# Linear attention and gated feed-forward: 23 identity products in the opening, and other slots for the attention work of the first looped pass

## Chip, cores and metric

One core of one Trainium2 chip. The metric is the device time of one execution in microseconds (us), the median over runs of the same program. A profile of one execution comes with it; its span is the time from its first to its last instruction.

## What is computed

Two stages, in float32:

```
state = 0                                   # per batch and head, 48 x 48
for t in range(768):                        # 4 batches, 8 heads of 48
    y[t]  = r[t] @ (state + (u * k[t]) outer v[t])
    state = w[t][:, None] * state + k[t] outer v[t]
x   = y as 3072 tokens x 384
out = (sigmoid(x @ w_gate) * (x @ w_val)) @ w_out      # 384 -> 1536 -> 384
```

## The kernel before, in words

**Groups and passes.** The 768 time steps of each batch are cut into 6 chunks of 128. A group q (0 to 23) is one chunk of one batch: batch q % 4, chunk q // 4. The four groups of one chunk make 512 tokens, which the feed-forward stage takes as one pass n (0 to 5). The 1536 hidden columns are 12 blocks f of 128.

**Attention work of a group.** `load_pin` and `load_tok` (L295, L304) fetch its two inputs by SyncE's queue into two buffers each, so a load waits until the group two places earlier has let go of its buffer. `bonus1`, `bonus2` and `bonus4` run on GpSimd (L317, L321, L328), `bonus3` on VectorE (L324). `prep_k` and `prep_r` (L334, L353) are scans and products on VectorE; `fade` (L347) scales the carried state. `guard` (L363) is ScalarE and reads what both scans wrote: `eg` has a single buffer. `turn_k` (L367) transposes the prepared keys on TensorE, `take_k` (L372) copies them out to `kT`, a single buffer. `section1` (L443) does the scores and sums on TensorE; `mask`, `middle` and `keep` (L456, L463, L471) follow on VectorE; `section2` (L448), or in the loops the weighing inside `both`, finishes the group. `take_y`, `turn_x`, `take_x`, `rest_x` turn the result into the feed-forward's operand, as a rounded part and a rest.

**Feed-forward step.** For each block f: `gate` (9 TensorE products of 128x128 by 512 columns, L525 and L528), `sigmoid` on ScalarE, `value` (9 products), `hidden` on VectorE (L545), `hidden_hi` on ScalarE (L549), `hidden_lo` on VectorE (L553), and, one step later, `down` (9 products, L568).

**Opening.** The class `Plan` simulates an order from costs given by hand for groups 0 to 7, for the twelve weight blocks (each is fetched and rebuilt from 64-bit words on VectorE, L269 to L287) and for pass 0. `section1(0)` and `section1(1)` lie in this part. Each engine runs its instructions in the order in which they are traced.

**Loops.** Passes 1 to 5 are written out as 12 steps of 4 slots; a dictionary `todo` hangs attention work on slots. Slot 0 comes ahead of `gate`, slot 1 ahead of `value`, slot 2 ahead of `down` of the step before, slot 3 behind it. `FIRST` gives the slots at which groups 8 to 11 are visited in pass 1. A visit `both(q)` does the end of group q and the scores and sums of group q+1 on TensorE, then `take_y(q)`, then mask, middle and keep of q+1, and it issues the loads of group q+2. `EARLY` holds, for each visit of pass 1, the slots at which group q+1 is prepared: first bonus1, bonus2, prep_k and fade; then turn_k and take_k; then prep_r and guard; then bonus3 and bonus4. In later passes the visits lie at slots 7, 19, 31 and 43 of the pass and these four at 7, 5, 3 and 3 slots ahead of the visit. Group 8 has turn_k at slot 1 and section1 at slot 3 of pass 1. Pass 1 also splits the last four weight blocks at slots 1 and 2, 5 and 6, 9 and 10, 13 and 14: `w_hi` (L284) on ScalarE, `w_lo` (L287) on VectorE.

```
row = 4 * NFF
start = (R0 + 1) * B
visit = {q: (q - start) // B * row + (7 + 12 * (q % B) if q >= start + B else FIRST[q - start]) for q in range(start, NG)}
at(1, turn_k, start)
at(1, take_k, start)
at(3, section1, start)
```

Of the kernel before, what the change touches and what calls it, by code (L numbers as in the profile page):

```python
# [9 lines left out]
F32 = mybir.dt.float32  # L10
# [11 lines left out]
P = 128  # L22
# [19 lines left out]
LATE = dict(b3=-1.05, wl=-28.0, xl=26.5)  # L42
ROOM = dict(pin=2, tok=2, bon=2, eg=1, ready=2, mid=1, kT=1, at=2, pair=1, bank=1, x=2, temp=1, pg=1, pu=1, unit=2)
R0 = 1
FIRST = [11, 21, 32, 43]
EARLY = [(4, 6, 8, 8), (12, 16, 17, 17), (23, 27, 28, 28), (34, 38, 39, 39)]
HC = C // 2
HALVES = [slice(0, HC), slice(HC, C)]
HW = 3 * DM // 2
# [155 lines left out]
def tile_kernel(ctx: ExitStack, tc: tile.TileContext, dec: bass.AP, tok: bass.AP, wts: bass.AP, u: bass.AP, out: bass.AP):  # L205
    nc = tc.nc
# [5 lines left out]
    ps1 = own.enter_context(tc.tile_pool(name="ps1", bufs=1, space=PSUM))  # L212
# [6 lines left out]
    def att_pair(name):  # L219
        return ps1.tile([P, 2, 512], F32, tag="pair", name=name)  # L220

    ident = const.tile([P, P], F32, name="ident")
# [85 lines left out]
    def kk(q):  # L308
        return pin[q][:, WW:WW + NP * C].rearrange("a (p c) -> a p c", c=C)

    def rr(q):
        return pin[q][:, WW + NP * C:].rearrange("a (p c) -> a p c", c=C)
# [63 lines left out]
    def values(q, p, o, half):  # L376
        h = 2 * p + o
        return tk[q][half, 2 * DM + h * D:2 * DM + (h + 1) * D]

    def scores(q):  # L380


        t = bank["a", q]
        todo = []
        for p in range(NP):
            for s, half in enumerate(HALVES):
                for o in range(2):
                    sl = slice(64 * o, 64 * o + D)
                    todo.append(lambda p=p, half=half, o=o, sl=sl: nc.tensor.matmul(  # L389
                        t[half, o, p * HC:(p + 1) * HC], lhsT=kk(q)[sl, p, half], rhs=rr(q)[sl, p, half], start=True, stop=True,  # L390
                        skip_group_check=True))
        return todo

    def sums(q):
        t = bank["a", q]
        todo = []
        for p in range(NP):
            for s, half in enumerate(HALVES):
                if s and q >= NG - B:
                    continue  # L400
                for o, m in ((0, 64), (1, D)):
                    todo.append(lambda p=p, s=s, half=half, o=o, m=m: nc.tensor.matmul(  # L402
                        t[64 * o:64 * o + m, s, NP * HC + p * D:NP * HC + (p + 1) * D],
                        lhsT=kT[q][half, p * L + 64 * o:p * L + 64 * o + m],
                        rhs=values(q, p, o, half), start=True, stop=True, skip_group_check=True))
        return todo
# [32 lines left out]
    def go(todo):  # L439
        for f in todo:  # L440
            f()

    def section1(q):  # L443

        bank["a", q] = att_pair(f"pa{q}")
        go(scores(q) + sums(q))

    def section2(q):  # L448


        t = att_pair(f"py{q}")
        bank["y", q] = [t[:, o, :NP * D].rearrange("a (p e) -> a p e", e=D) for o in range(2)]
        bank["yy", q] = t[:, :, :NP * D].rearrange("a o (p e) -> a o p e", e=D)
        go(among(*states(q, bank["y", q])) + among(*mix(q, bank["y", q])))
# [155 lines left out]
    for q in range(ahead + 2):  # L610
# [17 lines left out]
        add(f"tk{q}", "PE", 0.4, [f"pk{q}"], k + 0.1, turn_k, q, take=["bank", "kT"])  # L628
        add(f"kT{q}", "ACT", 0.53, [f"tk{q}"], k + 0.1, take_k, q, give=["bank"])
        add(f"s1_{q}", "PE", 1.3, [f"kT{q}", f"tok{q}", f"pr{q}"], k + 0.15, section1, q, take=["pair"], give=["kT"])  # L630
        add(f"mid{q}", "DVE" if old else "ACT", 0.36, [f"s1_{q}", old and f"fade{q}"], k + 0.1, middle, q, take=["mid"])
        add(f"mk{q}", "DVE", 0.7, [f"s1_{q}", f"b4_{q}"], k + 0.12, mask, q)
# [26 lines left out]
    for g, (i0, i1) in enumerate(GROUPS + [(0, B)]):  # L659
        m, some = i1 - i0, tall if g < 2 else WIDE  # L660
        for f in some:
            e = g == 0 or g == 1 and f in EXACT
            a, name = (0, f, i0, i1, e), f"{g}_{f}"
# [51 lines left out]
    def at(time, f, *a):  # L715
        todo.setdefault(time, []).append((f, a))

    def prepare(q, early, turn, late, more):
        at(early, bonus1, q)
        at(early, bonus2, q)  # L720
        at(early, prep_k, q)
        at(early, fade, q)
        at(turn, turn_k, q)
        at(turn, take_k, q)
        at(late, prep_r, q)
        at(late, guard, q)
        at(more, bonus3, q)
        at(more, bonus4, q)
# [8 lines left out]
# [5 lines that stand above are left out]
    settle(start, 3)  # L742
    for q, time in visit.items():
        if q + 1 < NG:
            prepare(q + 1, *EARLY[q - start] if q < start + B else (time - 7, time - 5, time - 3, time - 3))
        at(time, both, q)
# [78 lines left out]
```

## Time and profile before

| | before |
|---|---|
| runs, us | 582.59, 583.19, 584.51 (median 583.19) |
| profiled execution, us | 585.22 |
| its span, us | 582.9 |
| mean granted TensorE clock | 0.991 |
| TensorE products busy | 547.9 us, 94% |
| VectorE busy | 324.0 us, 56% |
| ScalarE busy | 204.7 us, 35% |
| GpSimd busy | 100.7 us, 17% |
| moved by DMA | 50.57 MB |

The profiled execution took 2.3 us more than its span, and 2.03 us more than the median of the runs. PE is TensorE's products, DVE VectorE, ACT ScalarE, POOL GpSimd, SPq SyncE's queue of DMA issues. Busy shares are means over stages with different limits; L numbers are lines of the kernel. In a timeline a line gives the start, the time until the end of the last of the merged instructions, and in square brackets how long the engine had been idle and what released it.

### The profile page before, as it was taken

Reading aid. Unit: us, or ns where it says so; the run is one execution under the profiler, and the core shown is the slowest. Engines: PE = TensorE matmul, PEld = TensorE weight load, DVE = VectorE, ACT = ScalarE, POOL = GpSimd, SP = SyncE. Lnnn points to the kernel's source line nnn. Section 1 sums busy time; section 2 is a strip of 40 time slices with the busy share of each in tenths; the row PEclk is TensorE's granted clock in tenths of the full one; section 3 lists DMA queues with packets and bytes.
Section 4 is the critical chain, followed back from the end, with each engine's and each line's share of the span. In section 5 each row is a group of like instructions: output and inputs, shape, how many; then the busy total and the mean of one; then the engine's idle time right before and its main releaser. Section 6 shows DMA issues by size and latency. Waiting matters only on the chain.

```text
span 582.9 us, 13165 instructions
## 1 busy us (share of the span) xinstructions
PE 547.9 (94%) x5864; PEld 449.3 (77%) x5864; DVE 324.0 (56%) x451; ACT 204.7 (35%) x376; POOL 100.7 (17%) x89
## 2 busy tenths in 40 slices
PE   3698899999889999999999999999999999999995
PEld 2577687887767888877888888888888888888884
DVE  4998999996754654644535545645545521222221
ACT  2557765744432323422223333223323322321221
POOL 4350533104010210210121221211220200000000
PEclk9999999999898999999999999999999999999998
DMA  8748827324020232231130330230330200100001
GB/s 253 256 170 284 251 93 305 76 77 147 12 90 15 76 89 60 84 90 40 51 90 12 110 113 13 77 90 15 112 107 19 72 3 1 55 1 1 0 1 60
DMA packets 11044, 50.57 MB, mean 87 GB/s; under 512 B 1265, under 2 KB 1266, under 8 KB 9442
## 3 DMA queue, kind: packets, MB, share of 16 engines
q1 hardware_dynamic: 8818, 45.70, 25.0%
q10 hardware_dynamic: 2160, 3.93, 1.7%
q8 instruction: 48, 0.79, 0.6%
q14 instruction: 18, 0.15, 0.1%
HBM read 44.91 MB, written 4.72 MB: 85 GB/s over the span
## 4 chain that ended last, share of the span: by engine, by line
PE 86%; DVE 6%; DMA 3%; issue 2%; ACT 1%; POOL 1%; SPq 0%; DVEq 0%; ACTq 0%
PE po L568 24%; PE pg L525 16%; PE pu L525 15%; PE pg L528 8%; PE pu L528 8%; PE py L431 3%; PE py L418 3%; DMA pin<-dec 3%; PE pg L522 2%; PE pk L370 2%; PE pa L389 2%; PE pa L402 1%; PE px L481 1%; DVE raw L275 1%; PE po L564 1%
## 5 line engine op out<-in xcount | busy, mean ns | idle before, releaser
L545 DVE TENSOR_TENSOR sg<-pu,sg 128x512 f32<-128x512 f32 (+1 forms) x76 | 50.3, 661 | 166.8 <-PE pu L528 162.1
L568 PE MATMUL po<-hh,w 128*128 128x512 f32 x408 | 130.3, 401 | 0.0
L525 PE MATMUL pg<-x,w 128*128 128x512 f32 x408 | 107.5, 399 | 0.0
L525 PE MATMUL pu<-x,w 128*128 128x512 f32 x408 | 105.0, 393 | 0.0
L525 PEld LDWEIGHTS pu<-x,w 128*128 128x128 f32 x408 | 76.8, 189 | 16.2
L525 PEld LDWEIGHTS pg<-x,w 128*128 128x128 f32 x408 | 74.9, 188 | 16.2
L568 PEld LDWEIGHTS po<-hh,w 128*128 128x128 f32 x408 | 75.1, 190 | 14.2
L549 ACT CAST hh<-sg 128x512 fp32r<-128x512 f32 x68 | 42.2, 620 | 123.0 <-DVE sg L545 122.9
L538 ACT ACTIVATE sg<-pg 128x512 f32<-128x512 f32 (+1 forms) x76 | 43.5, 572 | 115.2 <-PE pg L528 110.8
L568 PE MATMUL po<-hl,w 128*128 128x512 f32 x204 | 80.2, 393 | 0.1
L553 DVE TENSOR_TENSOR hl<-sg,hh 128x512 fp32r<-128x512 f32 x68 | 50.2, 738 | 42.2 <-ACT hh L549 42.2
L319 POOL TENSOR_TENSOR bon<-tok,ub 128x384 f32<-128x384 f32 x24 | 30.7, 1280 | 237.1 <-DMA tok<-tok 170.7
L528 PE MATMUL pg<-x,w 128*128 128x512 f32 x204 | 58.3, 394 | 0.0
L528 PE MATMUL pu<-x,w 128*128 128x512 f32 x204 | 57.6, 390 | 0.0
L332 POOL TENSOR_TENSOR at<-eye,a 128x512 f32<-128x512 f32 x24 | 31.5, 1314 | 126.2 <-DVE a L326 126.2
L568 PEld LDWEIGHTS po<-hl,w 128*128 128x128 f32 x204 | 38.6, 189 | 9.2 <-DVE hl L553 0.6
L528 PEld LDWEIGHTS pg<-x,w 128*128 128x128 f32 x204 | 38.7, 190 | 8.4
L528 PEld LDWEIGHTS pu<-x,w 128*128 128x128 f32 x204 | 38.3, 188 | 8.0
L339 DVE TENSOR_TENSOR_SCAN eg<-pin,ends 112x516 f32<-112x516 f32 x24 | 34.7, 1446 | 9.5 <-DMA pin<-dec 9.5
L365 ACT ACTIVATE eg<-eg 112x1032 f32<-112x1032 f32 x24 | 25.6, 1067 | 31.1 <-DVE pin L361 29.8
L322 POOL TENSOR_TENSOR bon<-bon,tok 128x384 f32<-128x384 f32 x24 | 35.5, 1480 | 1.9
L476 ACT COPY bon<-py 128x384 f32<-128x384 f32 x24 | 11.5, 478 | 63.7 <-PE py L431 63.7
(78 smaller groups left out, 646.5 us busy)
## 6 DMA issues: line engine op xcount, KB each, us to landing
pin<-dec SPq DMA_DIRECT2D x23, 675.5 KB, 5.9
tok<-tok SPq DMA_DIRECT2D x24, 576.0 KB, 5.8
raw<-wts SPq DMA_DIRECT2D x12, 1152.0 KB, 10.6
y<-o ACTq DMA_DIRECT2D x15, 256.0 KB, 2.0
y<-o SPq DMA_DIRECT2D x3, 256.0 KB, 3.2
pin<-dec SPq DMA_DIRECT2D x1, 448.0 KB, 3.8
pin<-dec SPq DMA_DIRECT2D x1, 227.5 KB, 2.8
line<-u SPq DMA_DIRECT2D x1, 1.5 KB
```

What stands on the lines that cost most here:

```text
L319: nc.gpsimd.tensor_tensor(out=bon[q], in0=tk[q][:, 0:DM], in1=ub, op=ALU.mult)
L322: nc.gpsimd.tensor_tensor(out=bon[q], in0=bon[q], in1=tk[q][:, DM:2 * DM], op=ALU.mult)
L332: nc.gpsimd.tensor_tensor(out=att[q], in0=eye.unsqueeze(1).unsqueeze(1).broadcast_to(shape), in1=a0, op=ALU.mult)
L339: nc.vector.tensor_tensor_scan(out=e[:, 516:0:-1], data0=t[:, 516:0:-1], data1=ends[:, 516:0:-1], initial=0.0, op0=ALU.mult, op1=ALU.add,)
L365: nc.scalar.activation(both, both, AF.Square, accum_out=acc_d[:, q:q + 1])
L525: nc.tensor.matmul(t, lhsT=w[f][:, cols], rhs=x[n][:, a, k, spot], start=k == 0 and j == 0, stop=False)
L528: nc.tensor.matmul(t, lhsT=whi[f][:, cols], rhs=x[n][:, 1, k, i0 * C:i1 * C], start=False, stop=k == NKT - 1)
L538: nc.scalar.activation(sg, hid["g", n, f, i0], AF.Sigmoid)
L545: nc.vector.tensor_tensor(out=sg, in0=hid["u", n, f, i0], in1=sg, op=ALU.mult)
L549: nc.scalar.copy(hh, hid["s", n, f, i0])
L553: nc.vector.tensor_tensor(out=hl, in0=hid["s", n, f, i0], in1=hid["hi", n, f, i0].bitcast(F32), op=ALU.subtract)
L568: nc.tensor.matmul(to, lhsT=w[f][:, cols], rhs=h, start=first and i == 0, stop=last and i == 2, skip_group_check=True)
```

## The change

Behind `section1` of groups 0 and 1, eleven and twelve products of the 128x128 identity with itself are issued into a bank (`po0`) that nothing reads until pass 0's first `down` starts a new sum there. In pass 1 the visits of groups 8, 9, 10 and 11 move from slots 11, 21, 32, 43 to slots 7, 19, 31, 43, and the preparation of groups 9 to 12 moves with them.

```diff
-FIRST = [11, 21, 32, 43]
-EARLY = [(4, 6, 8, 8), (12, 16, 17, 17), (23, 27, 28, 28), (34, 38, 39, 39)]
+BUSY = {0: 11, 1: 12}
+FIRST = [7, 19, 31, 43]
+EARLY = [(0, 2, 4, 4), (11, 14, 16, 16), (23, 26, 28, 28), (35, 38, 40, 40)]
...
         bank["a", q] = att_pair(f"pa{q}")
         go(scores(q) + sums(q))
+        if q in BUSY:
+            t = ps1.tile([P, 512], F32, tag="po0", name=f"busy{q}")
+            for _ in range(BUSY[q]):
+                nc.tensor.matmul(t[:, :P], lhsT=ident, rhs=ident, start=True, stop=True)
```

## Rows read from the trace of the kernel before

**Rows 1.** The page: granted clock in 40 slices; the chain's shares.
```profile
PEclk9999999999898999999999999999999999999998
...
PE 86%; DVE 6%; DMA 3%; issue 2%; ACT 1%; POOL 1%; SPq 0%; DVEq 0%; ACTq 0%
```

**Rows 2.** Windows: us; PE, PEld, DVE, ACT, POOL busy; PEclk, DMA share, GB/s.
```profile
153.00:157.00 4.00, 4.00 (x13) 3.33 (x14) 3.32 (x5) 1.05 (x2) 0.00 (x0) 0.57 0.01 4
...
175.50:181.00 5.50, 5.45 (x19) 4.45 (x20) 3.56 (x4) 2.12 (x4) 1.05 (x1) 0.69 0.01 3
181.00:262.00 81.00, 79.97 (x959) 65.83 (x958) 42.28 (x62) 23.31 (x47) 13.54 (x11) 1.00 0.25 75
262.00:576.00 314.00, 312.76 (x2921) 257.45 (x2919) 132.48 (x202) 85.57 (x164) 37.31 (x28) 1.00 0.15 46
```

**Rows 3.** Waits of TensorE over the whole span: total, times, longest.
```profile
PE py L431 <- issue: 3.4, 3, 1.3
```

**Rows 4.** Timeline of TensorE, pass 0's end and pass 1.
```profile
122.85 0.55 PE L370 MATMUL pk<-ident,pin 112*128 112x112 f32 x4
...
125.42 0.26 PE L418 MATMUL py<-ready,pin 48*64 48x48 f32 x2
...
152.95 0.95 PE L370 MATMUL pk<-ident,pin 112*128 112x112 f32 x4 [1.92 <-issue]
...
157.04 1.53 PE L525 MATMUL pg<-x,w 128*128 128x512 f32 x6
...
175.55 0.60 PE L370 MATMUL pk<-ident,pin 112*128 112x112 f32 x4 [3.12 <-DVE x L514]
...
181.74 0.62 PE L568 MATMUL po<-hh,w 128*128 128x512 f32 x2
...
199.01 0.55 PE L370 MATMUL pk<-ident,pin 112*128 112x112 f32 x4
...
203.53 0.62 PE L568 MATMUL po<-hh,w 128*128 128x512 f32 x2
```

**Rows 5.** Timeline of VectorE, then one line of GpSimd and of ScalarE, pass 1.
```profile
145.64 0.69 DVE L545 TENSOR_TENSOR sg<-pu,sg 128x512 f32<-128x512 f32 x1 [4.38 <-ACT sg L538]
...
150.83 1.22 DVE L339 TENSOR_TENSOR_SCAN eg<-pin,ends 112x516 f32<-112x516 f32 x1
...
152.18 0.66 DVE L345 TENSOR_TENSOR pin<-pin,eg 112x512 f32<-112x512 f32 x1
...
169.95 1.23 DVE L339 TENSOR_TENSOR_SCAN eg<-pin,ends 112x516 f32<-112x516 f32 x1 [3.55 <-DMA pin<-dec]
...
194.57 1.50 DVE L345 TENSOR_TENSOR pin<-pin,eg 112x512 f32<-112x512 f32 x1
...
194.51 1.01 POOL L319 TENSOR_TENSOR bon<-tok,ub 128x384 f32<-128x384 f32 x1 [14.29 <-DMA tok<-tok]
...
158.26 1.07 ACT L365 ACTIVATE eg<-eg 112x1032 f32<-112x1032 f32 x1 [3.47 <-DVE pin L361]
```

**Rows 6.** SyncE's queue (groups 9 and 10's loads), and the first one's landing.
```profile
136.86 28.39 SPq L301 DMA_DIRECT2D pin<-dec  x2
...
pin<-dec SPq DMA_DIRECT2D x1, 675.5 KB, 7.0
```

**Rows 7.** Timeline of TensorE, opening.
```profile
15.86 0.98 PE L370 MATMUL pk<-ident,pin 112*128 112x112 f32 x4 [5.20 <-DVE pin L345]
...
19.91 0.90 PE L481 MATMUL px<-ident,bon 128*128 128x128 f32 x3 [0.60 <-ACT bon L476]
...
25.92 1.09 PE L418 MATMUL py<-mid,pin 48*64 48x48 f32 x16 [3.23 <-DVE state L473]
...
48.24 0.49 PE L481 MATMUL px<-ident,bon 128*128 128x128 f32 x3
```

**Rows 8.** Timeline of VectorE, opening: the longest waits from 22 us on.
```profile
22.84 0.73 DVE L458 COPY_PREDICATED at<-after,pa 128x512 f32<-128x512 int32 x1 [1.08 <-PE pa L402]
...
52.77 1.23 DVE L339 TENSOR_TENSOR_SCAN eg<-pin,ends 112x516 f32<-112x516 f32 x1 [1.51 <-DMA pin<-dec]
```

## The prediction

> **What bounds the kernel now.** I read the chain first, then TensorE's waits, then the windows around each wait, then the other engines' timelines there. The chain is TensorE for 86% of the span [rows 1]. From 262 to 576 us its products are busy 312.76 of 314 us, from 181 to 262 us 79.97 of 81 [rows 2]; what is missing there is two of the three waits of L431 marked "issue", 3.4 us in all three [rows 3]. So whatever TensorE gains before 181 us moves the end by as much. Two stretches of pass 1 stand out, each a pause and then a slow clock:
> - 1.92 us ahead of turn_k(9) at 152.95 [rows 4]. VectorE finishes prep_k(9) just then: its scan starts at 150.83 and its product ends at 152.18 + 0.66 = 152.84 [rows 5]. Behind it the granted clock is 0.57 on the mean of 153 to 157 us [rows 2], that is, mostly the lower of its two levels, 1.2 instead of 2.4 GHz.
> - 3.12 us ahead of turn_k(10) at 175.55 [rows 4]. Here prep_k(10) began only at 169.95, after 3.55 us of waiting for its load [rows 5], and VectorE's queue did the rest. The clock behind it is 0.69 from 175.5 to 181 us [rows 2].
>
> The opening has the other pauses: 5.20 us ahead of turn_k(1) at 15.86 and 3.23 us ahead of section2(1) at 25.92 [rows 7]. The granted-clock line shows full speed there [rows 1], but three transposes take 0.90 us at 19.91 and 0.49 at 48.24 [rows 7], so by durations TensorE runs at its lower level through this stretch.
>
> **Pass 1: the visit of group 8 from slot 11 to 7, the preparation of 9 from (4, 6, 8, 8) to (0, 2, 4, 4), of 10 from (12, 16, 17, 17) to (11, 14, 16, 16).** No instruction is added or dropped; each visit's TensorE work is moved, not changed.
> - The pause at 152.95 goes: 1.92. Its slow clock: from turn_k(9) to the next gate 157.04 - 152.95 = 4.09 us for four transposes and nine products of down; the same work takes 125.42 - 122.85 = 2.57 at full clock [rows 4]. Saved 1.52.
> - The pause at 175.55 goes: 3.12. Its slow clock: turn_k, gate and value take 181.74 - 175.55 = 6.19, against 203.53 - 199.01 = 4.52 [rows 4]. Saved 1.67.
> - What is late next at turn_k(9). Its place is now right behind value(0), which is over when hidden(0) starts at 145.64; VectorE had idled 4.38 us before that [rows 5], so prep_k(9) and fade(9) fit there. But the load of group 9, issued at 136.86, lands 7.0 us later [rows 6], at 143.86. prep_k takes 152.84 - 150.83 = 2.01 and so ends at 145.87. I book a new wait of 0.5. hidden(0) slips behind prep_k and fade; its result is wanted by down(0), a whole gate and value later. take_k(9) must also wait for section1(8), which still reads the single kT buffer: that holds ScalarE for about a microsecond while its next work, sigmoid(1), has no input yet. Nothing.
> - What is late next at turn_k(10). Load 10 goes out with the visit, a step earlier than before, and has more than a step until slot 11: its 3.55 us of waiting goes. prep_k(10) stands on VectorE behind hidden(2), hidden_lo(2), rest_x(8) and w_lo(2), and is over, by the order above, some 0.4 us before value(3). I book 0 and keep 0.8 as the upper bound.
> - prep_r(9), bonus3(9), the mask of 9 and ScalarE's guard(9) stand a step earlier; their cover is the nine-product sums of TensorE beside them, and if it is gone the price is the last rival's. SyncE's loads of groups 10 and 11 move ahead with the visits and pass nothing else on that queue. GpSimd's two bonus products of 9 only waited for their load before and still do. The visits of 9, 10 and 11 move by 2, 1 and 0 slots into the pattern of the later passes, which run without pauses [rows 2]: nothing.
>
> Sum of pass 1: -1.92 - 1.52 - 3.12 - 1.67 + 0.5 = -7.7.
>
> [...] The product of prep_k took 0.66 alone and 1.50 where GpSimd's bonus product ran beside it, from 194.51 on [rows 5]. [...] Slot 0 puts both of group 9's there, but both hang on loads that land apart, so I leave it at 0.66; were they to meet, the new wait would be 1.50 - 0.66 = 0.84 longer, 1.3 instead of 0.5.
>
> **The opening: 11 and 12 products of 128 columns.** Nothing in the trace has this form. The nearest are the transposes by the identity, 0.90 / 3 = 0.30 each at the lower level, 0.49 / 3 = 0.16 at the upper [rows 7]. Eleven are 3.3 us in a pause of 5.20: hidden by the wait for prep_k(1). Twelve are 3.6 us in one of 3.23, hidden by the wait for keep(1), with 0.4 sticking out, or 2.0 at the upper level with nothing sticking out. Cost 0, bound 0.4. The bank is next written after the pauses, on the same engine.
>
> What a higher clock from there is worth is bounded by VectorE, which from 22 us on, until TensorE has the lead, waits only twice for over a microsecond: 1.08 us at 22.84 for section1(1)'s sums, and 1.51 at 52.77 for a load that is issued when TensorE lets a buffer go [rows 8]. Everything else that TensorE does faster before 33 us ends in front of a VectorE instruction that does not move. So the gain lies between 0 (or -0.4, the overhang) and 1.08 + 1.51 = 2.6. I take 1.0, the first wait: it is the nearest behind the first fill.
>
> Code-loading waits (the three of L431): the instruction stream shifts by 23 products, and such a wait may come or go, up to 1.3 each way [rows 3]. I take 0.
>
> **Sum.** -7.7 - 1.0 = -8.7. Against the profiled execution, 585.2, that is 576.5; it stands 2.03 above the median of the runs, so for the median 583.19 - 8.7 = 574.5.
>
> **Rivals.**
> 1. The identity products raise nothing that counts: the clock stays low until pass 0's dense products, or VectorE does not move. For it: dense small products already filled TensorE between the pauses and left it at the lower level. Against: these are full 128x128 products. 583.19 - 7.7 = 575.5.
> 2. One pause is moved, not removed: turn_k(9) waits longer for its load, or turn_k(10) for VectorE behind w_lo(2), long enough that the clock falls again. A pause of 1.92 had that effect, with 1.52 behind it [rows 4]. It costs 1.92 + 1.52 - 0.5 = 2.9: 577.4. For it: the margins are 0.5 and 0.4. Against: later passes keep the same distances.
> 3. Slower. At slot 4 guard(9) now stands on ScalarE ahead of sigmoid(1), and guard waits for prep_r on VectorE; before it waited 3.47 us there [rows 5]. If prep_r comes so late that sigmoid(1) frees the gate's bank after value(1), TensorE stops at each of the four visits of pass 1. At a pause and slow clock of 1.92 + 1.52 = 3.4 each, 13.8 in all, less 8.7: about 588. It decides from a delay of some 2 us, the length of value, and turns the sign at 2.2 us lost per visit. Against: guard stands the same way in the later passes, which show no pause.
>
> **How the numbers follow.** Forecast 0.45, 574.5; rival 1 0.30, 575.5; rival 2 0.20, 577.4; rival 3 0.05, 588. Low end: all of pass 1 without the new wait, 8.2, 2.6 in the opening and one code wait gone, 1.0: 583.2 - 11.8, about 571.5. High end: no gain in the opening, the first pause's 1.52 not in every run, both new waits (0.5 + 0.8) and a code wait of 1.3: 583.2 - 8.2 + 4.1, about 579. That holds all but rival 3 and some of rival 2's tail. A measurement tells 0.3% (1.7 us) from no change. Faster by more 0.95, within it 0.01, slower 0.04. The Trainium skill (TensorE: Matmul & The Clock Gate, Part 1) adds that one kernel met the faster clock after different numbers of products in different runs; by that the 1.52 and the opening's gain may vary from run to run. The runs before lie 1.9 us apart, which does not speak against it.
>
> **What would show it.** Right: no wait over 1 us at turn_k(9) and turn_k(10), clock 1.00 through pass 1, the pass shorter by 7 to 8 us; the transposes of group 0 near 0.49 instead of 0.90; VectorE's wait for section1(1) gone. Wrong: a pause at turn_k(9) with clock 0.5 behind it; sigmoid(1) late behind guard(9); transposes in the opening still at 0.90. A time under 571 would mean that the opening is not bound by VectorE as I read it; over 580, that the pauses moved on.

## The result and the profile after

The changed kernel takes 575.96 us (median of 4 runs, 575.17 to 577.14) against 582.89 of the kernel before on the same chip (4 runs, 582.03 to 584.51): 6.9 us less. The ratio on record is 0.9858, 95% interval [0.982, 0.9896], which is 8.3 us of the 583.19 that the prediction started from; the two medians alone give 0.9881, and the interval takes in both. Forecast were 574.5 and a range of 571.5 to 579.0. Timed again later beside other kernels, the ratio was 0.9858 [0.9819, 0.9897]. The profiled execution took 575.17 us with a span of 573.1; that of the kernel before had 582.9.

A line of the changed kernel's page, the clock by slices:

```profile
PEclk9799999999999999999999999999999999999999
```

Against [rows 1] the dip of the clock in the eleventh to thirteenth slice is gone, and a new one stands in the second slice, in the opening. The windows of the changed kernel (from:to and width in us; busy PE, PEld, DVE, ACT, POOL; PEclk, DMA share, GB/s) show both:

```profile
22.00:28.00 6.00, 6.00 (x47) 5.84 (x46) 4.95 (x6) 3.33 (x7) 0.70 (x1) 0.51 0.61 145
...
139.30:150.30 11.00, 10.55 (x110) 8.45 (x109) 7.38 (x12) 6.01 (x10) 1.77 (x2) 1.00 0.31 109
150.30:162.00 11.70, 11.70 (x203) 9.67 (x202) 7.27 (x13) 6.61 (x11) 2.09 (x2) 1.00 0.37 113
162.00:180.00 18.00, 17.38 (x228) 14.12 (x227) 11.98 (x16) 5.71 (x10) 3.27 (x3) 1.00 0.13 37
180.00:262.00 82.00, 82.00 (x822) 67.58 (x820) 44.28 (x65) 25.37 (x50) 15.57 (x12) 1.00 0.22 66
```

In pass 1 the clock is 1.00 throughout, where [rows 2] had 0.57 and 0.69. TensorE is missing 0.45 us of the window from 139.30 and 0.62 of that from 162.00. TensorE's waits in the changed kernel, over the whole span, name them (total, times, longest):

```profile
PE pa L403 <- issue: 2.7, 1, 2.7
PE pg L527 <- ACT sg L543: 1.4, 1, 1.4
...
PE py L432 <- issue: 1.0, 1, 1.0
...
PE pk L371 <- PE pu L533: 0.6, 1, 0.6
...
PE pk L371 <- ACT kT L375: 0.5, 1, 0.5
```

The two pauses of 1.92 and 3.12 [rows 4] have become 0.5 and 0.6. The waits of L431, now L432, are one of 1.0 instead of three of 3.4 [rows 3]. A wait of 2.7 in section1(1) is new, and so is one of 1.4 for the first sigmoid of pass 0: the faster TensorE of the opening gets there ahead of ScalarE. TensorE's timeline in the changed kernel (start, us, operation, the wait before it in brackets), first in the opening, then around pass 1:

```profile
10.60 4.42 PE L451 MATMUL busy<-ident 128*128 128x128 f32 x22
14.96 0.57 PE L371 MATMUL pk<-ident,pin 112*128 112x112 f32 x4
...
17.97 0.55 PE L486 MATMUL px<-ident,bon 128*128 128x128 f32 x3 [0.60 <-ACT bon L481]
...
18.96 0.32 PE L403 MATMUL pa<-tok,kT 64*64 64x48 f32 x9
21.98 0.88 PE L403 MATMUL pa<-tok,kT 64*64 64x48 f32 x23 [2.69 <-issue]
22.79 5.34 PE L451 MATMUL busy<-ident 128*128 128x128 f32 x24
28.06 0.67 PE L419 MATMUL py<-mid,pin 48*64 48x48 f32 x16
...
121.29 0.55 PE L371 MATMUL pk<-ident,pin 112*128 112x112 f32 x4
...
144.42 0.60 PE L371 MATMUL pk<-ident,pin 112*128 112x112 f32 x4 [0.45 <-ACT kT L375]
...
166.28 0.57 PE L371 MATMUL pk<-ident,pin 112*128 112x112 f32 x4 [0.62 <-PE pu L533]
...
194.68 0.61 PE L573 MATMUL po<-hh,w 128*128 128x512 f32 x2
```

The opening reads in this order: the first fill raises the clock (transposes 0.55 us instead of 0.90 [rows 7]); then TensorE stops for 2.69 us in the middle of a group of equal products; the clock falls, and the second fill runs at the lower level for 5.34 us, until section2(1) starts at 28.06 instead of 25.92 [rows 7].

Between the same two places, turn_k at 121.29 and the down sum at 194.68, lie 73.39 us. In the kernel before they were 203.53 - 122.85 = 80.68 [rows 4]. So 7.3 us of this pair of executions came from the visits of pass 1. Until the first of these places the changed kernel was 1.56 us ahead, and one code wait of the kernel before, 1.27 us, lies in that stretch. Two of its three lie behind 181 us, where the changed kernel has one.

### The profile page after: what moved, and what is told of

Read it like the earlier page. It is cut to its first block, busy times and chain, and to the rows that moved or that the text cites. A ratio compares the mean times of both kernels' runs of the same rounds, so it can differ in the third digit from the quotient of the medians.

```text
span 573.1 us, 13259 instructions
## 1 busy us (share of the span) xinstructions
PE 548.7 (96%) x5910; PEld 452.3 (79%) x5910; DVE 325.0 (57%) x451; ACT 204.3 (36%) x376; POOL 104.2 (18%) x89
## 4 chain that ended last, share of the span: by engine, by line
PE 83%; DVE 9%; issue 2%; ACT 2%; DMA 1%; POOL 1%; SPq 0%; ACTq 0%; DVEq 0%; POOLq 0%
PE po L573 23%; PE pg L530 16%; PE pu L530 15%; PE pu L533 8%; PE pg L533 8%; PE py L432 3%; PE py L419 3%; PE pa L403 1%; PE pa L390 1%; PE pk L371 1%; DMA tok<-tok 1%; DVE temp L273 1%; PE px L486 1%; DVE raw L276 1%; PE busy L451 1%
## 5 line engine op out<-in xcount | busy, mean ns | idle before, releaser
L558 DVE TENSOR_TENSOR hl<-sg,hh 128x512 fp32r<-128x512 f32 x68 | 51.9, 763 | 42.3 <-ACT hh L554 42.2
L320 POOL TENSOR_TENSOR bon<-tok,ub 128x384 f32<-128x384 f32 x24 | 29.2, 1215 | 230.5 <-DMA tok<-tok 199.2
L323 POOL TENSOR_TENSOR bon<-bon,tok 128x384 f32<-128x384 f32 x24 | 39.6, 1650 | 1.9
L340 DVE TENSOR_TENSOR_SCAN eg<-pin,ends 112x516 f32<-112x516 f32 x24 | 35.9, 1495 | 7.0 <-DMA pin<-dec 7.0
```

The costliest lines, as they stand in the source:

```text
L320: nc.gpsimd.tensor_tensor(out=bon[q], in0=tk[q][:, 0:DM], in1=ub, op=ALU.mult)
L323: nc.gpsimd.tensor_tensor(out=bon[q], in0=bon[q], in1=tk[q][:, DM:2 * DM], op=ALU.mult)
L340: nc.vector.tensor_tensor_scan(out=e[:, 516:0:-1], data0=t[:, 516:0:-1], data1=ends[:, 516:0:-1], initial=0.0, op0=ALU.mult, op1=ALU.add,)
L558: nc.vector.tensor_tensor(out=hl, in0=hid["s", n, f, i0], in1=hid["hi", n, f, i0].bitcast(F32), op=ALU.subtract)
```

## The experiments

Theory A: pass 1 carries the change, and the products matter little. Theory B: the products gain 2 us or more, by the clock in the opening. Theory C: they cost about as much as they bring. Theory D, formed after the first four runs: they gain because they shift TensorE's instruction stream, so that fewer code waits (the waits marked "issue" in the middle of a group of equal products) fall into the visits. Every kernel was timed against the kernel before on its chip; the table has the medians and the ratio to it. e1 to e4 ran on one chip, e5 to e12 on another, so the ratios compare better than the medians.

| run | edit | us | ratio, 95% |
|---|---|---|---|
| e1 | visits only | 578.09 | 0.9898 [0.9876, 0.9920] |
| e2 | products only | 581.03 | 0.9971 [0.9947, 0.9995] |
| e3 | visits, first fill | 576.80 | 0.9880 [0.9855, 0.9904] |
| e4 | visits, second fill | 577.47 | 0.9884 [0.9859, 0.9909] |
| e5 | second fill of 7 | 576.15 | 0.9874 [0.9842, 0.9906] |
| e6 | products of one column | 576.35 | 0.9884 [0.9849, 0.9918] |
| e7 | 3 and 3 products of 512 columns | 576.22 | 0.9877 [0.9845, 0.9909] |
| e8 | 24 more products of one column | 576.50 | 0.9877 [0.9840, 0.9915] |
| e9 | kernel before, group 9 prepared early | 582.70 | 0.9978 [0.9952, 1.0004] |
| e10 | group 10 prepared from slot 10 | 574.55 | 0.9844 [0.9801, 0.9886] |
| e11 | changed kernel again | 575.57 | 0.9858 [0.9819, 0.9897] |
| e12 | visits only again | 576.97 | 0.9890 [0.9848, 0.9932] |

**e1 and e12: the visits alone.**

```diff
-BUSY = {0: 11, 1: 12}
+BUSY = {}
```

> Only the visits of pass 1 are moved; no identity products. Theory A (pass 1 carries the change): between the first gate of pass 1 and the value product of its sixth step the changed kernel was 7.15 us shorter than the kernel before, so here some 6 to 8 us below the kernel before, 575 to 577, no pause over 1 us and clock 1.00 in pass 1. Theory B (the products carry a good part of it, by the clock in the opening): 2 us or more above the changed kernel, 578 or more. Theory C (the products cost more than they bring, since TensorE stood 2.69 us for code behind the first fill and section2(1) began at 28.06 instead of 25.92): equal to the changed kernel or up to 1.5 us below it.

> The visits-only kernel again, beside the changed one. Theories B and D: 1.5 to 2.5 us above it. Theory C: within 1 us.

The visits alone give 0.9898 and 0.9890, about 6 us of the kernel before. From turn_k in pass 0 to the same down sum the two profiles take 73.80 and 73.67 us, as the changed kernel's 73.39: pass 1 is settled. Theory A holds in its main point. TensorE's timeline of e12, these two places and the code waits behind them:

```profile
120.86 0.55 PE L371 MATMUL pk<-ident,pin 112*128 112x112 f32 x4
...
194.53 0.61 PE L573 MATMUL po<-hh,w 128*128 128x512 f32 x2
...
243.98 0.29 PE L432 MATMUL py<-tok,at 64*32 64x48 f32 x9 [1.41 <-issue]
...
267.43 0.23 PE L432 MATMUL py<-tok,at 64*32 64x48 f32 x1 [1.39 <-issue]
```

**e11: the changed kernel beside e12.**

> The changed kernel itself, timed beside the visits-only kernel on one chip. Theories B and D (the fills are worth some 2 us, by the clock or by the code waits): 1.5 to 2.5 us below the visits-only kernel. Theory C (they give about as much as they cost): within 1 us of it.

575.57 against 576.97: the products are worth 1.4 us here, 1.8 to 2.3 by the ratios (0.9890 and 0.9898 less 0.9858, of 583). By the medians that is between the theories' bounds, by the ratios it is what B and D expected; the intervals are 0.2 to 0.4% wide on each side, so only the sign is likely. The same places in TensorE's timeline of e11:

```profile
121.07 0.55 PE L371 MATMUL pk<-ident,pin 112*128 112x112 f32 x4
...
194.59 0.61 PE L573 MATMUL po<-hh,w 128*128 128x512 f32 x2
...
375.16 0.33 PE L432 MATMUL py<-tok,at 64*32 64x48 f32 x10 [1.76 <-issue]
```

So up to the down sum the products gained nothing: 194.59 with them, 194.53 without. Behind it the code waits are 1.76 us here and 1.41 + 1.39 = 2.80 in e12, and the spans, 573.6 and 574.5, differ by about as much. The changed kernel and e1 are much the same: both come to that sum at 194.68, then follow one wait of 0.99 against two of 1.33 and 1.40, 1.74 us less, and the spans are 573.1 and 574.4. Theory B's gain in the opening is not there in either pair.

**e2: the products alone.**

```diff
-FIRST = [7, 19, 31, 43]
-EARLY = [(0, 2, 4, 4), (11, 14, 16, 16), (23, 26, 28, 28), (35, 38, 40, 40)]
+FIRST = [11, 21, 32, 43]
+EARLY = [(4, 6, 8, 8), (12, 16, 17, 17), (23, 27, 28, 28), (34, 38, 39, 39)]
```

> Only the identity products; the visits stand where they stood before. Theory A: within 1.5 us of the kernel before, and both pauses of pass 1 (about 1.9 and 3.1 us) are there with the lower clock behind them. Theory B: 2 to 3 us below the kernel before. Theory C: 0 to 1.5 us above it. In each, section1(1) shows the code wait of some 2.7 us and the second fill runs at the lower level, about 5.3 us long.

1.7 us below the kernel before by the ratio, [0.3, 3.1]: between what A and B expected, and against C. Both pauses are there. What they do to the clock is not what I had read from one execution. TensorE's waits in e2 from 136 to 262 us:

```profile
PE pk L371 <- DVE x L519: 3.0, 1, 3.0
PE pk L371 <- issue: 1.9, 1, 1.9
```

The first belongs to turn_k(10), the second to turn_k(9). The windows of e2 around and behind each, columns as above:

```profile
146.00:151.00 5.00, 3.09 (x16) 2.33 (x16) 4.93 (x9) 1.84 (x2) 0.00 (x0) 1.00 0.01 2
151.00:156.00 5.00, 5.00 (x23) 4.10 (x23) 4.28 (x6) 1.32 (x3) 0.00 (x0) 1.00 0.00 0
...
168.00:174.00 6.00, 2.99 (x11) 2.29 (x10) 5.28 (x7) 1.63 (x4) 1.60 (x2) 0.69 0.01 1
174.00:180.00 6.00, 6.00 (x22) 4.77 (x21) 1.55 (x3) 2.07 (x4) 1.05 (x1) 0.74 0.00 0
```

Behind the same pause of 1.9 us the clock stays at 1.00 here; behind the 3.0 us it falls, and turn_k, gate and value take 178.57 - 171.32 = 7.25 us there, 2.73 more than the 4.52 at full clock [rows 4].

**e3 and e4: one fill each.**

```diff
-BUSY = {0: 11, 1: 12}
+BUSY = {0: 11}        # e3
+BUSY = {1: 12}        # e4
```

> The changed kernel without the twelve products of group 1. The code wait inside section1(1) stays (the eleven products ahead of it still shift the stream), the 5.3 us behind it go: section2(1) starts right behind keep(1), near 26.1 instead of 28.06, at the lower clock. Theory C: VectorE's wait of 0.98 for the first sigmoid of pass 0 shrinks and the kernel is up to 1 us faster than the changed one. Theory A: the same within 1 us, since VectorE is full again from 36 us on. Theory B: slower by 1 us or more, since the clock is no longer up ahead of pass 0.

> The changed kernel without the eleven products of group 0. The code boundary falls back to the end of section1(1), so no 2.7 us code wait there, but the section runs at the lower clock and ends near 22.7 as in the kernel before: VectorE's wait for it stays at 1.1 to 1.5. Then twelve products at 0.44 each take until about 28 and section2(1) is as late as in the changed kernel. Theory C: the same as the changed kernel within 0.5 us (the first fill is worth nothing, as code arrives no earlier). Theory B: 1 us slower or more.

Both lie between the visits alone and the whole change and apart from neither by their intervals. In e3 the code wait in section1(1) is 2.95 us and section2(1) runs at the lower level; in e4 there is none and the second fill ends the clock's lower level by itself. VectorE's wait for section1(1) is 2.4 us in e3 and 1.1 in e4: the first fill did not shorten it.

**e6, e7, e8, e5: time and instructions of the fills apart.**

```diff
-                nc.tensor.matmul(t[:, :P], lhsT=ident, rhs=ident, start=True, stop=True)
+                nc.tensor.matmul(t[:1, :1], lhsT=ident[:, :1], rhs=ident[:, :1], start=True, stop=True)  # e6
+                nc.tensor.matmul(t, lhsT=ident[:L], rhs=ends[:, :512], start=True, stop=True)            # e7, BUSY = {0: 3, 1: 3}
```

> The changed kernel with the same 11 and 12 products, each cut to one column by one column: the same number of TensorE instructions at the same places, and next to no time in them. Theory D (the fills gain by shifting TensorE's instruction stream, so that fewer of its code waits fall inside the visits: 3 of them, 3.4 and 3.1 us, in the kernel before and in the visits-only kernel, 1 of 1.0 to 1.1 us in the changed kernel and the fill-only one, 2 of 2.4 to 2.7 with either fill alone): one code wait of about 1 us in the visits, and the same time as the changed kernel within 0.7 us, although the opening stays at the lower clock. Theory B (they gain by the clock): section1(1) and section2(1) at the durations of the kernel before (1.04 to 1.5 us), and a time like the visits-only kernel's, 2 us above the changed one.

> The changed kernel with 3 and 3 products of 512 columns in place of 11 and 12 of 128: about the same time of TensorE and the clock up in the opening, but a quarter of the instructions (the stream is shifted by 6 products of two instructions and their loads instead of 23). Theory B: the same as the changed kernel within 0.7 us. Theory D: two or three code waits of 1 to 1.4 us in the visits, and 1.5 to 2 us slower than the changed kernel.

e8 keeps the fills and adds 24 products of one column behind the second; e5 has `BUSY = {0: 11, 1: 7}`.

> The changed kernel with 24 more products of one column behind the second fill: the stream is shifted by 24 more products, with little time in them. Theory D: the code waits in the visits change again in number or place; one more shift of this size took away one wait each time so far, so none is left and it is about 1 us faster than the changed kernel. Theory B: the same as the changed kernel or up to 1 us slower, for the time of the 24 products ahead of section2(1).

> The changed kernel with 7 products instead of 12 behind section1(1). At 0.44 us each (the twelve took 5.34 at the lower level) they end when keep(1) is done, so section2(1) starts near 26 instead of 28.06. Theory C: VectorE's wait of 0.98 for the first sigmoid goes and the kernel is up to 1 us faster. Theory D: that gain is within the scatter, and the stream is shifted 5 products less, so one or two code waits: the same or up to 1 us slower.

The four are equal within their intervals, and their ratios, 0.9874 to 0.9884, lie between the changed kernel's 0.9858 and the visits' 0.9890, apart from neither: by the times neither B nor D gets its verdict. In e5 VectorE's wait of 0.98 us for the first sigmoid is gone, as theory C had it, and the time did not fall. By the traces e6 speaks for D: the opening stays at the lower clock, and one code wait of 1.1 us is left in the visits. e7 speaks against D as I put it: with a quarter of the instructions it also has one, of 1.0. So does e8, which has one of 1.0, in pass 1, where D expected none.

What the traces do bear out of D is that the waits move with the instructions ahead of them. The first code wait behind pass 1 lies at 244 us without products (e1, e12), at 286 with the 12 instructions that e7's products show, at 310 with 22 (e3), 309 with 24 (e4), 352 with 36 (e5) and 374 to 375 with 46 (changed kernel, e6, e10, e11). That these waits are the products' 1.4 to 2 us is likely by the two pairs of profiles above; by the times it stays open.

These runs also show what the wait marked "issue" is. Section1(1) has 32 products of L403 (L402 before). TensorE's timeline around the wait in e1 (no fill), then in e7 (3 products ahead):

```profile
20.83 1.04 PE L403 MATMUL pa<-tok,kT 64*64 64x48 f32 x31
22.12 0.24 PE L403 MATMUL pa<-tok,kT 64*48 64x48 f32 x1 [0.26 <-issue]
```

```profile
17.81 0.55 PE L403 MATMUL pa<-tok,kT 64*64 64x48 f32 x25
20.36 0.45 PE L403 MATMUL pa<-tok,kT 64*64 64x48 f32 x7 [2.00 <-issue]
```

Without a fill the stop is behind 31 of them; with e7's three products, which the trace shows as six, behind 25; with eleven, shown as 22, behind 9. So it sits at a fixed count of instructions, wherever that falls, which I read as a wait for code; in the changed kernel the DMA queue of the kind "instruction" moves one packet between 18.5 and 20 us. Whether TensorE has to stop depends on when it gets there: 0.17 and 0.26 us at 21.4 and 21.9 (e12, e1), none in e6, which has the same 22 instructions ahead and gets there at about 21.6, but 2.00 to 2.95 us between 18.4 and 20.6, in the kernels with a first fill that takes time. Among those the sooner is not the longer: 2.00 at 18.4 in e7, 2.95 at 20.2 in e3. The DMA engines are full in that stretch (share 1.02 from 17 to 22 us in the changed kernel); that they hold the code up is not shown.

e8 shows how much the opening can hide. Its section2(1) starts at 30.02, VectorE then waits 2.9 us for pass 0's first value, and turn_k in pass 0 comes at 124.03, 2.7 us behind the changed kernel in this execution. The median of its runs shows nothing of it.

**e9: the first pause alone.**

```diff
-EARLY = [(4, 6, 8, 8), (12, 16, 17, 17), (23, 27, 28, 28), (34, 38, 39, 39)]
+EARLY = [(0, 2, 4, 4), (12, 16, 17, 17), (23, 27, 28, 28), (34, 38, 39, 39)]
```

> The kernel before with one edit: group 9 is prepared at slots (0, 2, 4, 4) instead of (4, 6, 8, 8); no visit is moved, no identity products. Theory A: the pause of 1.92 us ahead of turn_k(9) shrinks to the 0.5 to 0.7 us of the changed kernel (there ScalarE frees the bank late), the pause of some 3.1 us ahead of turn_k(10) stays with the lower clock behind it. The time falls by 1.2 to 1.5 us where the clock held behind the first pause, by up to 3 where it fell: 1.2 to 3 us below the kernel before. Rival: the first pause only moves to another place of the pass (the next late one is guard(9), which ScalarE waits for), and the time stays within 1 us of the kernel before.

1.3 us below the kernel before by the ratio, at the low end of what was expected, and the interval takes in no change and the rival's 1 us. In the profile the first pause is down to 0.6, and 0.5 appears at the gate that waits for sigmoid(1), which stands behind guard(9), the rival's place. TensorE's waits in e9 from 130 to 262 us:

```profile
PE pk L370 <- DVE x L514: 2.7, 1, 2.7
PE py L431 <- issue: 1.0, 1, 1.0
PE pk L370 <- ACT kT L374: 0.6, 1, 0.6
PE pg L525 <- ACT sg L538: 0.5, 1, 0.5
```

The windows of e9 around and behind the second pause, the 2.7 of the first row:

```profile
168.00:174.00 6.00, 3.34 (x17) 2.53 (x16) 5.28 (x7) 1.80 (x5) 1.91 (x2) 1.00 0.01 4
174.00:180.00 6.00, 6.00 (x39) 4.72 (x40) 1.99 (x4) 2.14 (x5) 1.05 (x1) 1.00 0.00 0
```

Here not even the pause of 2.7 us lowered the clock, and this execution, 578.94 us, was the shortest of its twelve (up to 586.04). It is not the usual one: its mean granted clock is 0.996, and nine of the twelve runs have 0.991 to 0.993.

**e10: group 10 ahead of w_lo(2).** In the changed kernel GpSimd and VectorE met at prep_k(10). Its GpSimd timeline there, then its VectorE timeline:

```profile
162.28 2.01 POOL L323 TENSOR_TENSOR bon<-bon,tok 128x384 f32<-128x384 f32 x1
```

```profile
161.71 1.71 DVE L288 TENSOR_TENSOR w<-raw,w 128x1152 fp32r<-128x1152 f32 x1
163.34 2.04 DVE L340 TENSOR_TENSOR_SCAN eg<-pin,ends 112x516 f32<-112x516 f32 x1
```

The scan takes 1.22 alone [rows 5], and w_lo 1.35. The edit:

```diff
-EARLY = [(0, 2, 4, 4), (11, 14, 16, 16), (23, 26, 28, 28), (35, 38, 40, 40)]
+EARLY = [(0, 2, 4, 4), (10, 14, 16, 16), (23, 26, 28, 28), (35, 38, 40, 40)]
```

> The changed kernel with group 10 prepared from slot 10 instead of 11, ahead of w_lo(2) on VectorE. In the changed kernel turn_k(10) waited 0.6 us: w_lo(2) stood ahead of prep_k(10), and the scan of prep_k(10) took 2.04 instead of 1.23 beside GpSimd's bonus product. Expected: prep_k(10) starts about 1.6 us earlier and the wait at turn_k(10) is gone, also if the scan still takes 2 us; 0.6 us faster than the changed kernel. Rival: w_lo(2), now behind prep_k(10), comes so late that the next block's work waits instead, and the time is the same.

VectorE's timeline of e10:

```profile
161.39 1.58 DVE L340 TENSOR_TENSOR_SCAN eg<-pin,ends 112x516 f32<-112x516 f32 x1
...
163.10 1.23 DVE L346 TENSOR_TENSOR pin<-pin,eg 112x512 f32<-112x512 f32 x1
...
164.52 1.34 DVE L288 TENSOR_TENSOR w<-raw,w 128x1152 fp32r<-128x1152 f32 x1
```

Its TensorE timeline, the two ends of the stretch:

```profile
121.07 0.55 PE L371 MATMUL pk<-ident,pin 112*128 112x112 f32 x4
...
193.53 0.62 PE L573 MATMUL po<-hh,w 128*128 128x512 f32 x2
```

The scan starts 2 us earlier, the wait at turn_k(10) is gone, and the stretch from turn_k in pass 0 to the down sum is 193.53 - 121.07 = 72.46 us, 0.9 below the changed kernel's 73.39 and 1.1 below e11's 73.52. GpSimd's products still meet prep_k(10): its scan takes 1.58 instead of 1.22 and its product 1.23 instead of 0.66 [rows 5]. The gain is from standing ahead of w_lo(2). The median is 1.0 below e11's. The intervals of the two ratios overlap, so the trace shows the gain and the times only suggest it. It has the lowest median of the kernels timed.

## Why the prediction was right

The forecast mechanism of pass 1 was right, the time 1.5 us above its centre and well inside the range. The clock's prices, the products' price and the wait at turn_k(10) were mis-sized. The term for the opening was wrong in its mechanism, and that the sum holds in spite of it is luck: pass 1 brought less than forecast, the products more, and not where I had it.

- **Pauses of pass 1, -1.92 and -3.12: right.** They are gone, and with -1.52 and -1.67 for the clock and the new waits the stretch got 7.3 us shorter in the two profiles (forecast 7.7).
- **The clock's prices, -1.52 and -1.67: mis-sized for the median.** They were read from one execution. In e2 they came to 0 behind the 1.9 us pause and 2.73 behind the 3.0, in e9 to 0 behind the 2.7. The visits alone brought 6.0 to 6.4 us by the ratio, not 7.7. How often the clock falls can be read from the runs timed with e1, which differs from the kernel before in pass 1 alone: the mean granted clock of the kernel before is 0.9929 over its 17 runs (0.988 to 0.998), that of e1 0.9967 over 6 (0.995 to 0.998), and 14 of the 17 lie below all of e1's. My estimate from the two means is 0.0038 of 580, 2.2 us, instead of 3.19. The prediction named this as a reason for its upper end ("the first pause's 1.52 not in every run") but kept both in the sum. The Trainium skill (TensorE: Matmul & The Clock Gate, Part 1) says that one kernel met the faster clock after different numbers of products in different runs; the runs here show such a scatter for the fall to the slower one.
- **"What is late next at turn_k(9)", 0.5: size right, cause wrong.** The load landed in time for prep_k(9) to start at 142.12 and end at 144.14. Last was the copy of take_k(8), which frees the bank for the next transposes and stood on ScalarE behind pass 0's three output copies. ScalarE's timeline in the changed kernel:

```profile
143.35 0.60 ACT L543 ACTIVATE sg<-pg 128x512 f32<-128x512 f32 x1 [0.41 <-ACT o L581]
143.84 0.53 ACT L375 COPY kT<-pk 128x448 f32<-128x448 f32 x1
```

- **"What is late next at turn_k(10)", 0 with 0.8 as the bound: 0.62.** Scan and w_lo ran beside GpSimd's products of the bonus: 2.04 instead of 1.22, and 1.71 instead of 1.35 (e10 has 1.34). The Trainium skill (SBUF — State Buffer, "Who interferes with whom") says that a VectorE instruction with two inputs in SBUF contends with a GpSimd instruction that reads there; the trace agrees, both being longer here. I had weighed it at the wrong place, turn_k(9), where the two did not meet.
- **Rival 3: did not decide, but its wait is real.** guard(9) waited 4.47 us for prep_r, with sigmoid(1) behind it; the gate's bank came free in time. ScalarE's timeline in the changed kernel:

```profile
151.23 1.07 ACT L366 ACTIVATE eg<-eg 112x1032 f32<-112x1032 f32 x1 [4.47 <-DVE pin L362]
...
152.29 0.58 ACT L543 ACTIVATE sg<-pg 128x512 f32<-128x512 f32 x1
```

- **The opening, -1.0: did not come about; luck covered it.** I took VectorE's wait of 1.08 for section1(1) as the gain. It grew, as VectorE's timeline in the changed kernel shows:

```profile
22.98 0.73 DVE L463 COPY_PREDICATED at<-after,pa 128x512 f32<-128x512 int32 x1 [1.51 <-PE pa L403]
```

The clock did rise behind the first fill, but the faster TensorE ran into the code wait of 2.69 us and later waited 1.4 for a sigmoid. Turn_k in pass 0 came at 121.29 and 121.07 us with the products, at 120.88 and 120.86 without them (over all ten profiles with products from 119.7 to 124.0): as in rival 1, nothing that counts was raised there. What the products bring, 1.4 to 2.3 us over the whole kernel, lies behind pass 1 in the profiles, where the code waits are 1.0 and 1.8 us instead of 2.7 and 2.8. The code-loading term, set to 0, was what moved.
- **The products' price: too low.** A product of the identity is two instructions in the trace (x22, x24), not one like a transpose: 4.42 and 5.34 us instead of the 3.3 and 3.6 that I took. The second fill stuck out by some 2 us instead of 0.4.

## What to carry to other kernels

Here a pause of 2 to 3 us ahead of a dense TensorE stage cost itself each time, and the slower clock behind it in most executions, not in all: count the pause in full and the clock as part of the range, and look at the granted clock of all runs before taking a price from one profile. When preparation is moved a slot forward, look at what each queue holds ahead of it and at whether a GpSimd product will meet it on VectorE; a place ahead of one more VectorE instruction (e10) ended the wait at turn_k(10). Filler products are not free where code arrives late: here they moved a code wait of 2.7 us into the opening.

## What the runs showed of the hardware that was not expected

The same pause lowered TensorE's clock in one execution and not in another: 1.92 us with 0.57 behind it [rows 2] and 1.9 with 1.00 (e2); 3.0 with 0.69 (e2) and 2.7 with 1.00 (e9). Over 17 runs of the kernel before, the mean granted clock went from 0.988 to 0.998.

The stop that I read as TensorE's wait for code sat at a fixed instruction count (behind 31, 25 and 9 of the same 32 products, for 0, 3 and 11 products ahead of them). It took 0.17 to 0.26 us where TensorE came to it at 21.4 us or later, and 2.00 to 2.95 where it came at 20.6 or sooner.
